# Pieces of a split exponential in single buffers, some of them made in place by an accumulating DMA, in a kernel for gated full and sliding-window attention

## The chip, the core and the metric

The kernel runs on one core of a Trainium2 chip. It is written for five engines: TensorE (PE: matmuls), VectorE (DVE), ScalarE (ACT: exponentials), GpSimd (POOL) and SyncE (SP, which issues DMA transfers). Data lies in SBUF (128 partitions); matmuls write to PSUM, which has eight banks of 512 float32 columns. The metric is the device time of one execution in microseconds, the median over several.

## The reference

Inputs are one sequence x of 2048 rows of 512, two sets of attention weights A and B, and a gate vector. All are bfloat16; there are 32 heads of 16 columns.

```python
x = A_x
g = sigmoid((x * gate_w).sum(-1, keepdims=True))
# A: full attention
qkv = (x @ A_wqkv).reshape(B, S, 3, H, Dh) ...
p = softmax(einsum("bhqd,bhkd->bhqk", q, k) * Dh ** -0.5)
a = einsum("bhqk,bhkd->bhqd", p, v).reshape(B, S, D) @ A_wo
# B: each row sees 8 keys, 2 rows apart, at and before itself
b = ... @ B_wo
out = g * a + (1 - g) * b
```

Nearly all of the work is in A: 32 heads with 2048 x 2048 scores each, whose exponentials are needed.

## The kernel before

**Items and blocks.** A's scores are cut into 2048 items. An item is one head, 128 keys and 512 queries: one matmul of 128 x 512 scores into one PSUM bank, 128 x 512 exponentials, and then one or more matmuls with V (with a column of ones beside it, which gives the softmax's denominator). Four heads run side by side on the four strips of the PE array. 64 items are a block (four heads, one stretch of 512 queries, 16 key tiles); there are 32 blocks. At a block's end its accumulator bank is normalised (`norm_steps`), and later the output projections follow (`outproj_specs`, and `outproj_last` for the last two tiles of rows).

**Two ways to make an exponential.** ACT takes items two or three banks at a time from two PSUM slots (banks 0 to 2 and 3 to 4): L1926 writes the tile `pt`, and one matmul per item with V follows (L1645, `pt,vaug`). The third bank of the wide slot can be lent out, and then ACT's exponential has two banks. DVE takes single items of certain key tiles (`KD`) in the remaining banks, by a sum of three pieces. A piece is a linear map of the score, written as int16 and read by PE as fp16, which makes a piecewise linear power of two; the three pieces are shifted against each other by thirds of an octave, and V is multiplied beforehand by the weights `PW_W` (tiles `vaug`, `vaugw`). So such an item has three matmuls with V, which sum in PSUM.

**How the three pieces are made.** DVE makes piece 0 from PSUM, item by item (`exp_dve`, L1564). Up to four items form a batch. When a batch is closed (`close_batch`), pieces 1 and 2 of the whole batch are made from piece 0 by adding an integer constant: on DVE (L1573) or on POOL (L1571, which adds two int16 at a time as int32, to a constant in the tile `pc`). The tile `yb` holds all three pieces of a batch; there are three such tiles (`NYB`), and one comes free when all of its 12 matmuls with V are done.

**Who decides the order.** The whole kernel is laid out when it is built. `run` keeps an estimate of the time on each engine (`t`), with a cost for each kind of step (`T_ACT`, `T_D1`, `T_D4`, `T_PI` and so on), and at each point picks what the engine that is furthest behind does next: the score matmuls of the next slot, matmuls with V whose pieces are thought ready, or another step (projections, branch B, output projections). Each engine then runs its instructions in that order, and semaphores make it wait where something isn't ready. The picks depend on limits: `TUNE` has places and due times in items, and `LEVELS` with `STRETCH` give twelve limits a level in each of 64 stretches of the run.

**Branch B** is spread through the same order: projections, logits by products and matmuls, and from some 375 us on transfers (`er`, `erb`, `vw`, issued by SP) and products on POOL (L1360). POOL also does the scaling of V (L930), part of the normalisation (L1678) and, early, squares of x (L1180). It issues two transfers: `woB` (L1153) and `woA`, which lies in the tile `wAv` (L1151).

**POOL and DVE.** When the planner puts a step on POOL, it makes it wait for the last DVE step marked `port` (L1573 pieces, products), and it holds such DVE steps back while it believes POOL to be busy.

Of the kernel before, what the change touches and what calls it, by code (L numbers as in the profile page):

```python
# [9 lines left out]
ALU = mybir.AluOpType  # L10
# [3 lines left out]
F16 = mybir.dt.float16  # L14
# [26 lines left out]
PW_S = tuple(s - math.log2(3.127444) for s in (0.0, -0.3330078125, 0.3330078125))  # L41
NP_ = len(PW_S)
KD = (2, 4, 7, 9, 12, 14)
KZ = (9,)
# [3 lines left out]
NPT = (4, 4)  # L48
NYB = 3
NQM = 3  # L50
# [4 lines left out]

TUNE = dict(relL=64, dueL2=2040, R0=74, R1w=42, R1g=20, R2g=31, R3g=46, R3w=50, dueB=61, dueL=84, v2rel=79, v2step=21, v2due=91, krel=230, krel2=192, ahead=0.142, dueV=30, dueS=115, dueO=678, dlast=62, qrel=28, prelB=59, prodrel=-12)

LEVELS = dict(
    pool=(0.0, 0.4, 1.2, 2.5, 4.0),
    backlog=(0.758, 1.231, 1.61, 1.894, 2.273, 2.841, 3.788),  # L60
    backlog_s=(0.888, 1.442, 1.886, 2.219, 2.663, 3.329, 4.438),
    part_us=(0.6, 0.975, 1.275, 1.5, 1.8, 2.25, 3.0),
    misc_slack=(-32, -18, -12, -8, -4, 2, 16),
    urgent=(-25, -11, -5, -1, 3, 9, 23),
    fit=(0.0, 0.2, 0.3, 0.4, 0.5, 0.6, 0.8),
    port=(0.338, 0.549, 0.718, 0.845, 1.014, 1.268, 1.69),
    alone=(-8.973, -0.273, -0.123, 0.027, 0.177, 0.327, 9.027),
    grab=(1, 0, 2, 3, 4),
    lend=(1, 0, 2, 3, 4, 5, 6, 7),
    order=((-1, 0, 1, 2, 1), (-1, 1, 0, 2, 3), (-1, 0, 2, 1, 3), (-1, 0, 1, 2, 3), (1, 0, 1, 2, 3), (0, 0, 1, 2, 3), (1, 0, 2, 1, 3), (2, 0, 1, 2, 3)),  # L70
)
STRETCH = dict(
    pool="1343344333433432333333333333232333333333333330333301233333333333",
    backlog="3333333333133333333333333333633333663333433463333133346332333333",
    backlog_s="3330413333333333333333323333033331333333631333333333331333332333",
    part_us="6333115334333333333333333533333333333643633330333335333333363303",
    misc_slack="3336333333533323333333333333333333333033333323333333433333303333",
    urgent="3341331533633333332533333333333333333333333303333333230333033331",
    fit="3613335633413353333333330333333111333333333340323333031333133333",
    port="3333533433333333333333332333333333435333333333333333333533333333",  # L80
    alone="2333333333333303333323333313333335133533303333333333333333333333",
    grab="0004204000034000030000003000000000000300000040000000300000000300",
    lend="0001000200000010000000000600000000000000000000401000006000020000",
    order="3003600020460000000144002001060007000000600020000000500060072000",
)
# [636 lines left out]
T_P1 = lambda n: n / 390.0 + 0.2  # L722
T_PI = lambda n: n / 1150.0 + 0.12
T_P2 = lambda n: n / 470.0 + 0.065
MM = 0.216
# [29 lines left out]
class _Fast:  # L755
# [15 lines left out]
    def setup(self):  # L771
# [17 lines left out]
                   for a, (w, n) in enumerate(zip(ACT_W, NPT))]  # L789
        self.yb = [c([P, NP_, YB_ITEMS * 512], I16, name=f"yb{i}") for i in range(NYB)]  # L790
        self.oT = [c([P, S], BF16, name=f"oT{i}") for i in range(2)]
# [76 lines left out]
        nc.gpsimd.memset(self.halo[:], 0.0)  # L868
        for k in range(1, NP_):
            nc.gpsimd.memset(self.pc[:, k:k + 1], round(1024.0 * (PW_S[k] - PW_S[0])) * 65537)  # L870
        self.idx = pidx, pf, ei, ef
# [616 lines left out]
    def run(self):  # L1488
# [17 lines left out]
        pt_refs = {}  # L1506
        yb_free = [0.0] * NYB
        batch = None
# [27 lines left out]
        def cold(now):  # L1536
            return sum(n for a, n in work if a > now - WARM_WIN) < WARM_BAR
# [23 lines left out]
        def exp_dve(slot_item):  # L1561
            (b, kt, j), bt, i, bank = slot_item
            A = SCALE * math.log2(math.e) * 1024.0
            return nc.vector.tensor_scalar(out=self.yb[bt["buf"]][:, 0, i * 512:(i + 1) * 512], in0=bank[:],  # L1564
                                           scalar1=A, scalar2=1024.0 * (15.0 + PW_S[0]), op0=ALU.mult, op1=ALU.add)

        def piece(bt, k, gp=False):
            n = len(bt["items"]) * 512
            y = self.yb[bt["buf"]]
            if gp:  # L1570
                return nc.gpsimd.tensor_tensor(out=y[:, k, 0:n].bitcast(I32), in0=y[:, 0, 0:n].bitcast(I32),  # L1571
                                               in1=self.pc[:, k:k + 1].to_broadcast([P, n // 2]), op=ALU.add)
            return nc.vector.tensor_scalar(out=y[:, k, 0:n], in0=y[:, 0, 0:n],  # L1573
                                    scalar1=float(round(1024.0 * (PW_S[k] - PW_S[0]))), scalar2=None, op0=ALU.add)

        def close_batch():
            nonlocal batch
            bt = batch
            batch = None
            n = len(bt["items"]) * 512  # L1580
            bt["refs"] = NP_ * len(bt["items"])
            parts = [dict(n=NP_) for _ in bt["items"]]

            def done(k, end):
                for i, it in enumerate(bt["items"]):
                    add_pv(it, self.yb[bt["buf"]][:, k, i * 512:(i + 1) * 512].bitcast(F16), end, ("y", bt, k), parts[i])
            now = min(t.values())
            pl = max(0.0, t["POOL"] - now) + sum(s.cost for s in self.steps if s.eng == "POOL" and s.rel <= p
                                                 and ready_time(s) <= now + 1.0)
            for k in range(1, NP_):  # L1590
                gp = pl < tune("pool") and n >= 1024
                pl += gp * T_PI(n)
                s = Step("POOL" if gp else "DVE", T_PI(n) if gp else T_D4(n), lambda k=k, gp=gp: piece(bt, k, gp),
                         deps=list(bt["p1"]), due=bt["due"], cls=2)
                s.on_done = lambda end, k=k: done(k, end)
                s.port = not gp
                self.steps.append(s)
            last = bt["p1"][-1]

            def after(end, prev=last.on_done):  # L1600
                prev(end)
                done(0, end)
            if last.end is None:
                last.on_done = after
            else:
                done(0, last.end)

# [8 lines left out]
        def emit_pv_one(j, now):  # L1616
# [13 lines left out]
            if kind == "p":  # L1630
                pt_refs[ref] -= 1
                if pt_refs[ref] == 0:
                    pt_free[ref] = now + 0.45
            else:
                ref["refs"] -= 1
                if ref["refs"] == 0:
                    yb_free[ref["buf"]] = now + 0.45
            out = self.flex[acc[b]][32 * j:32 * j + 32, :]
# [131 lines left out]
        def d_wanted(now, flex=True):  # L1770

            if p >= N - 8 or p % 64 >= TUNE["dlast"] or not any(k in KD for r in rem[p // 64] for k in r):
                return False
            if batch is None and min(yb_free) > now:
                return False
            if flex and min(fx_free) > now:
                return False
            ready = [s for s in self.steps if s.rel <= p and s.eng in ("PE", "DVE") and ready_time(s) <= now + TUNE["ahead"]]
            if flex and any(s.acq and s.due <= p + tune("misc_slack") for s in ready):
                return False  # L1780
            load = max(0.0, t["DVE"] - now) + sum(s.cost for s in ready if s.eng == "DVE")
            return load < tune("backlog" if flex else "backlog_s")
# [29 lines left out]
        def d_add(it, bank, p1done):  # L1812
# [3 lines left out]
            if batch is None:  # L1816
                buf = min(range(NYB), key=lambda i: yb_free[i])
                batch = dict(buf=buf, items=[], p1=[], due=0.0, blk=b)
                yb_free[buf] = INF
            bt = batch  # L1820
# [31 lines left out]
        def emit_alone(d, now):  # L1852
# [10 lines left out]
            d0.end = t["PE"] + 0.25  # L1863
            if batch is not None and p < N and p - 64 * batch["blk"] >= TUNE["dlast"]:
                close_batch()

        def emit_qk(dv, ac, now):
# [12 lines left out]
            for d in dv:  # L1880
                d[2].end = t["PE"] + 0.25
            if batch is not None and p < N and p - 64 * batch["blk"] >= TUNE["dlast"]:
                close_batch()
# [3 lines left out]
        while True:  # L1887
# [80 lines left out]
            else:  # L1968
# [27 lines left out]
                else:  # L1996
# [21 lines left out]
                    full = len(av) == 4  # L2018
                    part = av and (free_p <= 1 or min(yb_free) > now + 0.5 or cold(now) or now - old > tune("part_us") or (cur == NB - 1 and left[cur] <= len({(e[1], j) for j, q in enumerate(pvq) for e in q})) or p >= N)
                    pick = None  # L2020
# [93 lines left out]
```

## Time and profile before

| | |
|---|---|
| median of 3 runs | 703.62 us (702.6 to 704.75) |
| the profiled execution | 702.96 us |
| its span, first to last instruction | 701.2 us |
| mean granted clock of TensorE | 0.997 |
| exponentials on ACT: with 2 banks, with 3 banks | 582, 100 |
| items on DVE (L1564) | 584, mean 681 ns |
| pieces on DVE (L1573), on POOL (L1571) | 206, 104 |
| transfers that POOL issues | 2 |
| DMA, mean over the span | 69 GB/s |

How to read it: the span is what the sum of the prediction is made against. The busy time of an engine is the union of its instructions' spans, and a mean duration holds the time that an instruction spends beside its neighbour on the same engine. An arrow names who ended the idle time of an engine.

### The profile page before, as it was taken

What the parts mean: (1) busy time and instruction counts of PE and PEld (TensorE: products, weight loads), DVE (VectorE), ACT (ScalarE), POOL (GpSimd) and SP (SyncE); (2) the same over time, 40 slices, a digit from 0 to 9 for tenths busy, and PEclk for the clock granted to TensorE, in tenths of its full rate; (3) what the DMA queues carried; (4) which work ended last, traced back from release to release, by engine and by line L of the source; (5) the groups of instructions that cost most, each with busy time, mean ns of one, the idle gap of its engine ahead of it and who ended that gap; (6) DMA issues with size and microseconds to landing.
All of it is one profiled execution on the core that took longest, in us unless ns stands there. A gap on an engine that the chain in (4) does not pass through costs nothing.

```text
span 701.2 us, 21328 instructions
## 1 busy us (share of the span) xinstructions
PE 679.4 (97%) x8556; PEld 218.0 (31%) x8556; DVE 651.8 (93%) x1093; ACT 680.5 (97%) x696; POOL 429.1 (61%) x364
## 2 busy tenths in 40 slices
PE   9999999999999999999998999999999999999996
PEld 4432222233322232223332223322333232232343
DVE  6999999997899999999999899999999999989983
ACT  6999999999999999999999999999999999999995
POOL 4766877766476455555456666666567564576681
PEclk9999999999999999999999999999999999999999
DMA  6001101000100100000103236356463554566531
GB/s 175 5 16 36 45 3 31 2 2 9 35 2 15 26 1 5 6 2 9 34 1 92 99 79 165 106 146 162 96 156 97 149 134 112 128 167 173 136 84 36
DMA packets 64489, 48.70 MB, mean 69 GB/s; under 512 B 22528, under 2 KB 64000, under 8 KB 64256
## 3 DMA queue, kind: packets, MB, share of 16 engines
q1 hardware_dynamic: 63680, 45.83, 25.2%
q8 instruction: 69, 1.13, 0.7%
q0 software_dynamic: 288, 1.05, 0.5%
q10 hardware_dynamic: 416, 0.39, 0.2%
q14 instruction: 36, 0.29, 0.2%
HBM read 39.85 MB, written 5.26 MB: 64 GB/s over the span
## 4 chain that ended last, share of the span: by engine, by line
PE 60%; ACT 22%; issue 6%; DVE 5%; DMA 3%; SPq 2%; POOL 1%; ACTq 0%; DVEq 0%; POOLq 0%
ACT pt L1926 22%; PE fps L1872 21%; PE fps L1645 20%; PE fps L895 15%; DVE yb L1564 2%; DMA vw<-v_dram 1%; PE fps L1857 1%; SPq L1328 1%; PE fps L1378 1%; DVE yb L1573 1%; DMA erb<-er_dram 1%; DVE prod L1229 1%; SPq L968 1%; DMA x_in<-in_A_x_dram 1%; ACT er L1248 0%
## 5 line engine op out<-in xcount | busy, mean ns | idle before, releaser
L1926 ACT ACTIVATE pt<-fps 128x1024 bf16<-128x1024 f32 (+1 forms) x682 | 674.5, 1141 | 7.8 <-PE fps L1872 5.6
L1564 DVE TENSOR_SCALAR yb<-fps 128x512 int16<-128x512 f32 x584 | 377.8, 681 | 18.4 <-PE fps L1872 15.3
L1872 PE MATMUL fps<-qm,kT 32*128 32x512 bf16 x1976 | 285.9, 383 | 12.6 <-ACT pt L1926 7.8
L1645 PE MATMUL fps<-pt,vaug 128*32 128x512 bf16 (+1 forms) x1562 | 234.7, 373 | 0.4 <-DVE yb L1564 0.4
L1571 POOL TENSOR_TENSOR yb<-yb,pc 128x1024 int32<-128x1024 int32 (+1 forms) x104 | 188.4, 1822 | 64.6 <-DVE yb L1573 15.2
L1645 PE MATMUL fps<-yb,vaugw 128*32 128x512 f16 (+1 forms) x1228 | 174.6, 375 | 0.6 <-POOL yb L1571 0.4
L1872 PEld LDWEIGHTS <-kT 32*128 32x128 bf16 x1976 | 80.9, 91 | 272.2 <-issue 267.2
L1573 DVE TENSOR_SCALAR yb<-yb 128x2048 int16<-128x2048 int16 (+3 forms) x206 | 132.5, 670 | 0.6
L1645 PE MATMUL fps<-yb,vaug 128*32 128x512 f16 (+1 forms) x614 | 113.0, 375 | 0.0
L1360 POOL TENSOR_TENSOR er<-er,vw 128x512 bf16<-128x512 bf16 x64 | 72.8, 1156 | 49.7 <-DVE yb L1573 30.6
L895 PE MATMUL fps<-xT,ww 128*32 128x512 bf16 (+2 forms) x1296 | 99.5, 380 | 0.2
L1360 POOL TENSOR_TENSOR erb<-erb,vw 128x512 bf16<-128x512 bf16 x64 | 72.5, 1156 | 38.4 <-DVE yb L1573 20.6
L1645 PEld LDWEIGHTS <-vaug 128*32 128x32 bf16 x2176 | 64.8, 94 | 81.6 <-issue 74.7
L1645 PEld LDWEIGHTS <-vaugw 128*32 128x32 bf16 x1228 | 45.1, 94 | 41.8 <-issue 35.1
L1229 POOL TENSOR_TENSOR prod<-bq,bk 128x512 bf16<-128x512 bf16 x32 | 34.3, 1075 | 31.4 <-DVE yb L1573 17.4
L895 PEld LDWEIGHTS <-ww 128*32 128x32 bf16 x1296 | 25.8, 95 | 31.6 <-issue 23.8
L1678 POOL TENSOR_TENSOR t<-t,rc 128x512 bf16<-128x512 f32 x15 | 15.8, 1056 | 27.0 <-DVE yb L1573 12.2
L930 POOL TENSOR_SCALAR vaugw<-vaug 128x128 bf16<-128x128 bf16 (+1 forms) x24 | 20.4, 852 | 18.5 <-DVE vaug L923 10.8
L1857 PE MATMUL fps<-qm,kz 128*32 128x512 bf16 x288 | 30.8, 383 | 0.6 <-DVE yb L1564 0.4
L1229 DVE TENSOR_TENSOR prod<-bq,bk 128x2048 bf16<-128x2048 bf16 x24 | 29.9, 1271 | 0.2
L1668 DVE STREAM_TRANSPOSE t<-fps 128x512 f32<-128x512 f32 x32 | 22.7, 708 | 2.3 <-PE fps L1645 1.9
L895 PE MATMUL fps<-woB,oB 128*32 128x512 bf16 x256 | 19.9, 382 | 0.0
(117 smaller groups left out, 306.0 us busy)
## 6 DMA issues: line engine op xcount, KB each, us to landing
vw<-v_dram SPq DMA_DIRECT2D x128, 128.0 KB, 3.2
er<-er_dram SPq DMA_DIRECT2D x128, 64.0 KB, 3.3
erb<-er_dram SPq DMA_DIRECT2D x128, 64.0 KB, 2.9
v_dram<-vs SPq DMA_DIRECT2D x16, 128.0 KB, 2.6
qm<-qs SPq DMA_DIRECT2D x112, 16.0 KB, 1.8
out_dram<-ob SPq DMA_DIRECT2D x13, 128.0 KB, 2.7
x_in<-in_A_x_dram SPq DMA_DIRECT2D x3, 512.0 KB, 6.2
ww<-in_B_wqkv_dram SPq DMA_DIRECT2D x12, 128.0 KB, 2.8
```

Source lines behind the costliest of these rows:

```text
L895: self.nc.tensor.matmul(out=out_ps[32 * c:32 * c + 32, 0:n], lhsT=lhsT_of(c), rhs=rhs, start=start, stop=stop, tile_position=(0, 32 * c))
L930: return self.nc.gpsimd.tensor_scalar(out=self.vw4[k][:, KD.index(st), h0:h1, 0:DH], in0=self.vaug4[:, st, h0:h1, 0:DH], scalar1=PW_W[k], ...
L1229: return e.tensor_tensor(out=pr[m % 2][:, a:b], in0=bq[ct][:, a:b], in1=bk[ct][:, o + a:o + b], op=ALU.mult)
L1360: return nc.gpsimd.tensor_tensor(out=st_["erb"][m % 4][:, g, :], in0=st_["erb"][m % 4][:, g, :], in1=st_["vw"][m % 2][:, g, :], op=ALU.mult)
L1564: return nc.vector.tensor_scalar(out=self.yb[bt["buf"]][:, 0, i * 512:(i + 1) * 512], in0=bank[:], scalar1=A, scalar2=1024.0 * (15.0 + PW_ ...
L1571: return nc.gpsimd.tensor_tensor(out=y[:, k, 0:n].bitcast(I32), in0=y[:, 0, 0:n].bitcast(I32), in1=self.pc[:, k:k + 1].to_broadcast([P, n ...
L1573: return nc.vector.tensor_scalar(out=y[:, k, 0:n], in0=y[:, 0, 0:n], scalar1=float(round(1024.0 * (PW_S[k] - PW_S[0]))), scalar2=None, op0 ...
L1645: nc.tensor.matmul(out=out, lhsT=v, rhs=r, start=start, stop=stop, tile_position=(0, 32 * j))
L1668: nc.vector.transpose(out=self.t1[:, par].rearrange("p a b -> p (a b)"), in_=self.flex[acc[b]])
L1857: nc.tensor.matmul(out=dst[32 * c:32 * c + 32, :], lhsT=self.kz[:, j, KZ.index(kt), 32 * c:32 * c + 32], rhs=self.qm[(4 * ct + qc) % NQM][ ...
L1872: nc.tensor.matmul(out=dst, lhsT=self.kT[ct % 2][32 * j:32 * j + 32, kt * 128:(kt + 1) * 128], rhs=self.qm[(4 * ct + qc) % NQM][par][32 * ...
L1926: nc.scalar.activation(out=self.pt[pi[0]][pi[1]][:, 0:n * 512], in_=self.aslot[si][:, 0:n, :].rearrange("p a b -> p (a b)"), func=ACT.Exp, ...
```

## The change

The three-piece tile `yb` becomes eight single buffers `ys` of one piece of a batch each (`NSL`), and a constant tile `step` is added. DVE now makes the middle piece first (piece 1, by the shift `PW_S[1]`). The other two are made in one of two ways:

- fresh: a copy with a constant added into another buffer, on DVE or POOL, as before;
- in place: once every matmul and every copy that reads the buffer is done, POOL issues a DMA that adds the tile `step` to it (`accum_op=ALU.add`, 128 x 2048 int16, 512 KB for a full batch). The buffer then holds the next piece. A buffer can be changed twice so: piece 1, then 0, then 2, each step by the same constant.

How many of the two are fresh depends on the place in the block (the new limits `acc1`, `acc2`) and on the buffers that are free at that time: early in a block both can be made in place, later one, towards the end none. The planner counts such a transfer with 0.9 us on POOL, 1.8 in the queue for a full batch and 2.3 to its landing (5.0 from item 1100 on).

A batch is also closed at the very end of the items (`p < N` is dropped in two places). Ten values of `TUNE` and all of `LEVELS` and `STRETCH` are new, with fewer 3-bank exponentials and a different order throughout as a consequence. Branch B and the head and tail are changed only in their places.

```diff
+STEP_OF = {k: round(1024.0 * (PW_S[k] - PW_S[1])) for k in (0, 2)}
...
-NYB = 3
+NSL = 8
...
-TUNE = dict(relL=64, dueL2=2040, R0=74, R1w=42, R1g=20, R2g=31, R3g=46, R3w=50, dueB=61, dueL=84, v2rel=79, v2step=21, v2due=91, krel=230, krel2=192, ahead=0.142, dueV=30, dueS=115, dueO=678, dlast=62, qrel=28, prelB=59, prodrel=-12)
+TUNE = dict(relL=20, dueL2=2040, R0=110, R1w=42, R1g=12, R2g=31, R3g=43, R3w=50, dueB=61, dueL=84, v2rel=79, v2step=21, v2due=91, krel=230, krel2=214, ahead=0.142, dueV=-9, dueS=100, dueO=665, dlast=62, qrel=32, prelB=27, prodrel=-12)
 LEVELS = dict(
...
+    acc1=(-37, 11, 19, 27, 35, 43, 91),
+    acc2=(-57, -9, -1, 7, 15, 23, 71),
...
+ACC_B, T_ALB = 1100, 5.0
+T_AI, T_AQ, T_AL = 0.9, 1.8, 2.3
...
-        self.yb = [c([P, NP_, YB_ITEMS * 512], I16, name=f"yb{i}") for i in range(NYB)]
+        self.ys = [c([P, YB_ITEMS * 512], I16, name=f"ys{i}") for i in range(NSL)]
+        self.step = c([P, YB_ITEMS * 512], I16, name="step")
...
+        nc.gpsimd.memset(self.step[:].bitcast(I32), STEP_OF[0] * 65537)
...
+        def slice_dec(bt, sl, at):
+            bt["cnt"][sl] -= 1
+            bt["at"] = max(bt["at"], at)
+            if bt["cnt"][sl]:
+                return
+            if sl != bt["buf"] or not bt["ip"]:
+                ys_free[sl] = bt["at"] if sl == bt["buf"] else at
+                return
+            k = bt["ip"].pop(0)
...
+            def acc():
+                nonlocal acc_q
+                acc_q = max(acc_q, t["POOL"] + T_AI) + T_AQ * n / 2048
+                s.lat = acc_q + (T_AL if p < ACC_B else T_ALB) - t["POOL"] - T_AI
+                return nc.gpsimd.dma_start(out=self.ys[sl][:, 0:n], in_=self.step[:, 0:n], accum_op=ALU.add)
+            s = Step("POOL", T_AI, acc, deps=[d0], due=bt["due"], cls=2)
+            s.on_done = lambda end: bt["done"](k, sl, end)
...
+            pos = p - 64 * bt["blk"]
+            sls = sorted((i for i in range(NSL) if ys_free[i] <= now), key=lambda i: ys_free[i])[:NP_ - 1]
+            want = (pos >= tune("acc1")) + (pos >= tune("acc2"))
+            fresh = [2, 0][:min(len(sls), want)]
+            bt["ip"] = [k for k in (0, 2) if k not in fresh]
...
-            if batch is None and min(yb_free) > now:
+            if batch is None and sum(x <= now for x in ys_free) < 2:
...
-            if batch is not None and p < N and p - 64 * batch["blk"] >= TUNE["dlast"]:
+            if batch is not None and p - 64 * batch["blk"] >= TUNE["dlast"]:
```

## The prediction

> **What bounds the kernel now.** I read the page's busy shares first, then the groups by line and shape, then who waited for whom on ACT and PE, and last the rows around the two places where ACT stood still.
>
> ```profile
> span 701.2 us, 21328 instructions
> PE 679.4 (97%) x8556; PEld 218.0 (31%) x8556; DVE 651.8 (93%) x1093; ACT 680.5 (97%) x696; POOL 429.1 (61%) x364
> ...
> L1926 ACT ACTIVATE pt<-fps 128x1024 bf16<-128x1024 f32 (+1 forms) x682 | 674.5, 1141 | 7.8 <-PE fps L1872 5.6
> ```
>
> The groups by line with shapes kept apart (busy, mean ns of one, idle before):
>
> ```profile
> L1926 ACT ACTIVATE pt<-fps 128x1024 bf16<-128x1024 f32 x582 | 555.5, 1077 | 4.2 <-PE fps L1872 2.6 <-PE fps L1645 0.7 <-ACT pt L1926 0.2
> L1926 ACT ACTIVATE pt<-fps 128x1536 bf16<-128x1536 f32 x100 | 150.8, 1508 | 3.6 <-PE fps L1872 3.0 <-ACT pt L1926 0.2
> L1573 DVE TENSOR_SCALAR yb<-yb 128x2048 int16<-128x2048 int16 x178 | 121.8, 707 | 0.5
> L1571 POOL TENSOR_TENSOR yb<-yb,pc 128x1024 int32<-128x1024 int32 x94 | 176.8, 1891 | 59.5 <-DVE yb L1573 13.9 <-DVE yb L1564 13.5 <-PE fps L1872 10.2
> ```
>
> ACT's exponentials (L1926) fill 674.5 of 701.2 us with 7.8 us idle before them in the whole run. Neighbours overlap, so the mean of one is no price. The two widths differ by 1508 - 1077 = 431 ns, and 582a + 100(a + 0.431) = 674.5 gives a = 0.926 us for a two-bank exponential and 1.357 for a three-bank one. PE waits little for ACT (7.8 us at L1872), so the two are nearly level. DVE and POOL matter only where something of theirs comes late. The waits of ACT after the head are few:
>
> ```profile
> ACT pt L1926 <- PE fps L1872: 3.2, 7, 1.4
> ACT pt L1926 <- PE fps L1645: 0.7, 2, 0.3
> ACT pt L1926 <- ACT pt L1926: 0.4, 2, 0.2
> ```
>
> That is 4.3 us between 20 and 690 us. One event makes 1.97 of it:
>
> ```profile
> 384.50 0.40 PE L1872 MATMUL fps<-qm,kT 32*128 32x512 bf16 x4 [1.56 <-DVE yb L1564]
> 385.02 2.36 ACT L1926 ACTIVATE pt<-fps 128x1536 bf16<-128x1536 f32 x2 [0.59 <-PE fps L1872]
> ...
> 388.01 0.61 PE L1872 MATMUL fps<-qm,kT 32*128 32x512 bf16 x4
> 388.76 2.37 ACT L1926 ACTIVATE pt<-fps 128x1536 bf16<-128x1536 f32 x2 [1.38 <-PE fps L1872]
> ```
>
> PE waited 1.56 us for DVE. ACT lost 0.59 at once and 1.38 later, because PE's matmuls took 0.61 instead of 0.40 us for about 3 us (the granted clock is 0.83 in that slice of 10 us). A PE wait of that size costs ACT about 2 us.
>
> **The change, part by part.** Counts are from the built order of both programs, prices from rows.
>
> *ACT.* Two-bank exponentials go from 582 to 646, three-bank from 100 to 55, and one of one bank is new: 1464 banks become 1458, in 20 more instructions. 646 x 0.926 + 55 x 1.357 + 0.495 = 673.3, so -1.2 us. The last two exponentials shrink from three and two banks to two and one, which is 0.9 of that 1.2. On the path, up to the exponential that frees the bank for the last score matmul, only -0.3 is left.
>
> *The tail.* Behind the last score matmul PE had 64 matmuls of 512 columns and 52 of 256; now it has 112 and 20, as output projections have moved back. 16 matmuls take 1.05 us and 8 take 0.61, so one is 0.055 and a short one 0.0275: 4.95 us becomes 6.71, +1.76, all on the path. The normalisation of the last block (2.2 us on DVE) stays hidden behind 60 matmuls (3.3 us). Without them it would cost up to 2.2.
>
> *The head.* In the first 15 exponentials eight are of three banks instead of three. ACT lost 0.28 + 1.63 + 0.23 + 0.33 = 2.5 us there to PE's start-up work. Eight transposes (0.6 less 0.16 of switching, about 0.45 us) move from the 1.63 us gap to ahead of the first score matmul, so that part is a wash; the wider exponentials can cover the two small gaps. I take -0.5, bounds 0 and -2.5.
>
> *DVE.* Pieces made on DVE (L1573) fall from 206 to 153: 43 x 0.707 + 3 x 0.435 + 4 x 0.555 + 3 x 0.293 = 34.8 us less. Six more first exponentials (L1564) at 377.8/584 = 0.647 give back 3.9. DVE is 31 us lighter, and it is not the bound, so this counts only where PE waits for it. I take the event at 384 us as gone (-2.0); bounds 0 (it falls elsewhere) and -4.3 (every wait listed above).
>
> *POOL.* Its additions (L1571) fall by 33 x 1.891 + 3 x 1.464 + 3 x 1.037 = 69.9 us. New are 90 accumulating transfers, which POOL issues, and one memset of the step tile (about 1.0, like L860) in an idle stretch of the head. The nearest rows are the two plain 512 KB loads that POOL issues:
>
> ```profile
> 76.98 1.31 POOL L1153 DMA_DIRECT2D woB<-in_B_wo_dram  x1
> 77.29 0.69 DVE L1573 TENSOR_SCALAR yb<-yb 128x2048 int16<-128x2048 int16 x1
> 176.01 0.81 POOL L1151 DMA_DIRECT2D wAv<-in_A_wo_dram  x1
> ```
>
> and, from the list of transfers (KB each, us from issue to landing):
>
> ```profile
> woB<-in_B_wo_dram POOLq DMA_DIRECT2D x1, 512.0 KB, 4.6
> wAv<-in_A_wo_dram POOLq DMA_DIRECT2D x1, 512.0 KB, 4.6
> qm<-qs SPq DMA_DIRECT2D x112, 16.0 KB, 1.8
> ```
>
> 90 issues at 0.81 to 1.31 are 73 to 118 us, so POOL ends 3 to 48 us busier than 429 of 701, which its idle time covers.
>
> *The new wait.* An accumulation waits on POOL for the last matmul that reads the buffer. Queued behind it are branch B's products (er, erb), the normalisation product and the vaugw scaling, all 1.1 us pieces with due times many microseconds out. Its consumer is a probability-times-V matmul on PE, behind which the next score matmuls stand, and ACT behind those. So the question is whether the transfer lands before its consumer's turn. I counted, for each of the 90, the exponentials that stand between the releasing matmul and the consumer, at 0.926 and 1.357: 5.1 us for the tightest, seven of 5.6, two of 6.0, eleven of 6.4 to 6.5, six of 6.8 to 6.9, thirty others of up to 15.7 in the first half; 7.8 and up for the last 33. Lower price: 4.6, a plain load. Upper price: a 16 KB transfer lands in 1.8, so size made 2.8 of the 4.6; the accumulation also reads its destination, and doubling that part gives 7.4. I take 5.1, near the plain rows, since bytes and queue are the same: nobody is late, 0 us. At 7.4, 30 of the first 57 are late.
>
> A rule speaks against this. A load issued beside a DVE piece copy held POOL 1.31 us, one beside other DVE work 0.81: 0.50 us by the rows. The Trainium skill, page "SBUF — State Buffer", sections "SBUF: two separate sides" and "A bandwidth-pool intuition that's wrong (but worth ruling out)", says that VectorE in a two-port mode locks GpSimd out of writing descriptors, so that a transfer of 620 ns took 3100. An estimate by that page would put 2.5 us on each issue that meets such a copy, 7.1 instead of 5.1, and make those with the least slack 1 to 2 us late; the trace shows the effect at a fifth of that size.
>
> **Sum.** 701.2 - 0.3 + 1.76 - 0.5 - 2.0 + 0 = 700.2 us of span. The profiled execution took 702.96, 1.76 more than its span, and the median of the runs shown is 703.62, 0.66 above it: 700.2 + 1.76 + 0.66 = 702.6. The runs of before spread from 702.6 to 704.75; 0.3% (2.1 us) is about what a measurement of this kernel can tell from no change, so this is none.
>
> **The rivals.**
>
> *A: no change (0.36).* ACT's sum is equal to 0.2%, the tail's loss eats the head's and DVE's gain. For it: 4.3 us of idle time is all there is to win. Against: 90 new waits are unlikely to cost exactly nothing. 702.6, its own range 701.5 to 705.7.
>
> *B: faster (0.32).* With DVE 31 us lighter, nearly all of ACT's waits go: -4.3 instead of -2.0, and the head gives its -2.5. 701.2 - 0.3 + 1.76 - 2.5 - 4.3 = 695.9, so 698.3; half way there it is 700.4. For it: DVE stood at 49.6 of 50 us between 250 and 350 us, where its lateness starts. Against: those stretches have ACT at 50.0 of 50 already.
>
> *C: slower (0.32).* The accumulations land late and PE stands at their consumers. ACT has about one exponential (0.9 us) in hand, so it decides from a landing of 5.6 + 0.9 = 6.5 us after the release. At 7.4 the losses beyond 0.9 are 1.4 for the tightest, 7 x 0.9, 2 x 0.5 and next to nothing for the rest: 8.7 us, 708.9 in place of 700.2, or 711.3. Each PE wait near 1.5 us also risks the slower matmuls seen at 388 us, so more is possible. For it: the accumulating form is in no row, and POOL, in order, may be inside a 1.89 us addition when a buffer is released. Against: the slack listed, and loads of the same bytes at 4.6.
>
> *D: the change doesn't do what it says.* Then no accumulation would be in the order, but 90 of 308 pieces are. What is true of it is that they save ACT only six banks; the time would then be A's. It gets no chance of its own.
>
> **How the numbers follow.** A has the most and gives 702.6. B ends at 698.3 at its best, so the low end is 698. C at the upper price is 711.3; most of it lies under, and I put the high end at 710. That leaves out some 0.05 below and 0.13 above. Faster 0.32, same 0.36, slower 0.32 are B, A and C.
>
> **What would show it.** Right: the exponentials' group at 673 us; an interval of about 5 us from PE's last score matmul to ACT's closing copy growing to about 7; POOL's transfers landing in 4.6 to 5.5; no PE wait on them in the waits. Wrong: landings over 6.5, PE idle before L1690 put down to ys or to POOL, slices of granted clock under 1.0 beyond the one at 380 to 390 us, or ACT idle time after 20 us far from 2 us.

## The result and the profile after

The changed kernel takes 756.28 us (median of 4 runs, 754.23 to 761.15) against 704.18 (4 runs, 702.6 to 704.84): ratio 1.0753, 95% interval 1.0692 to 1.0815, so it is slower by 52 us. The prediction was 702.6 with a range up to 710. Its rival C, accumulations that land late, named a part of the mechanism and priced it far too low, at 711.3.

The page of the changed kernel is that of its slowest run (761.15 us). It shows its span, PE's busy share, the granted clock in 40 slices, the DMA queue of POOL (packets, MB, share), the groups of the exponentials, of the matmuls that read a buffer changed in place, and of the accumulations themselves (busy, mean ns | idle before), and their transfers (KB, us from issue to landing):

```profile
span 759.3 us, 21354 instructions
...
PE 706.2 (93%) x8531; PEld 219.9 (29%) x8531; DVE 642.2 (85%) x1046; ACT 686.9 (90%) x716; POOL 443.5 (58%) x416
...
PEclk9999999999999998999999999999989999898899
...
q0 software_dynamic: 13248, 47.19, 32.6%
...
L1971 ACT ACTIVATE pt<-fps 128x1024 bf16<-128x1024 f32 (+1 forms) x702 | 680.7, 1097 | 55.9 <-PE fps L1917 52.0
...
L1604 POOL DMA_DIRECT2D ys<-step x90 | 80.9, 954 | 55.8 <-PE fps L1917 31.7
...
L1690 PE MATMUL fps<-ys,vaug 128*32 128x512 f16 (+1 forms) x620 | 86.2, 387 | 22.6 <-DMA ys<-step 20.9
...
ys<-step POOLq DMA_DIRECT2D x86, 512.0 KB, 5.7
```

ACT was the bound and had 7.8 us of idle time before its exponentials. Now it has 55.9, and 52.0 of it is ended by a score matmul. PE in turn stands. Its waits in the changed kernel (total, times, longest):

```profile
PE fps L1690 <- DMA ys<-step: 21.4, 21, 2.7
...
PE fps L1917 <- DVE vs L1345: 4.2, 4, 2.0
```

The second row has a transfer behind it that is no accumulation. DVE writes the tile `vs` of branch B, and it stands until an earlier `vs` has been copied out; the kernel before has no such wait:

```profile
DVE vs L1345 <- DMA v_dram<-vs: 14.9, 7, 6.0
```

21 of the 90 accumulations make PE wait, 21.4 us in all, yet ACT loses more than twice that. One event shows how. POOL's rows, from when four accumulations follow each other (start, duration, idle before):

```profile
271.26 1.75 POOL L1604 DMA_DIRECT2D ys<-step  x2 [1.96 <-PE fps L1690]
273.88 0.85 POOL L1604 DMA_DIRECT2D ys<-step  x1 [0.87 <-DVE ys L1584]
...
275.43 1.19 POOL L1604 DMA_DIRECT2D ys<-step  x1
```

The first row holds two issues, at 271.26 and 271.84. The transfers issued at 271.84, 273.88 and 275.43 land 6.65, 7.3 and 9.71 us later. They share the engines, and the four landings are 2.7 to 4.0 us apart. The same stretch on PE:

```profile
281.22 0.40 PE L1690 MATMUL fps<-ys,vaug 128*32 128x512 f16 x4 [0.55 <-DMA ys<-step]
281.55 0.60 PE L1917 MATMUL fps<-qm,kT 32*128 32x512 bf16 x5
282.08 0.40 PE L1690 MATMUL fps<-pt,vaug 128*32 128x512 bf16 x4
285.18 0.62 PE L1690 MATMUL fps<-ys,vaug 128*32 128x512 f16 x4 [2.70 <-DMA ys<-step]
```

A row merges neighbouring instructions: the five of 281.55 take 0.38 us each. So after the wait of 0.55 us the matmuls keep their speed, and after that of 2.70 us they take about 0.6 us instead of 0.39, until 290.2. Two windows of 10 us (busy time of PE, weight loads, DVE, ACT, POOL; then granted clock, DMA share, GB/s):

```profile
270.00:280.00 10.00, 9.41 (x103) 2.88 (x101) 8.72 (x13) 9.68 (x10) 4.50 (x5) 1.00 1.02 191
280.00:290.00 10.00, 6.72 (x87) 1.89 (x85) 5.81 (x11) 6.38 (x8) 4.04 (x5) 0.68 0.61 117
```

In the first the DMA engines are full (1.02, 191 GB/s); in the second the clock is 0.68 and ACT works 6.38 of 10 us. So a PE wait of this length is paid twice, once standing and once slow.

**A measure for all runs.** From each exponential's start to the next one's I subtract a fixed step, 0.916 us for two banks and 1.343 for three (the median steps of the kernel before are 0.904 and 1.331). What is left is ACT's excess; other fixed steps would shift all rows nearly alike. Before it is 16.8 us in all, after 72.2. The sum of fixed steps is nearly equal (666.5 and 665.6). Adding the first exponential (+1.6 us later) and the stretch behind the last one (+2.5), these four terms give the span's +58.1 within 0.5: 55.4 of it is excess. It lies in both halves of the run:

| run | time, us | ratio (95%) | fixed steps | excess before 400 us | from 400 us | PE waits for accumulations |
|---|---|---|---|---|---|---|
| before | 704.2 | 1 | 666.5 | 13.5 | 3.4 | - |
| after | 756.3 | 1.0753 (1.0692 to 1.0815) | 665.6 | 31.2 | 41.0 | 21.4 |
| e1_sixteen | 708.7 | 1.0067 (1.0047 to 1.0087) | 665.6 | 13.9 | 5.0 | 0 |
| e2_plain | 727.7 | 1.0323 (1.0285 to 1.0361) | 665.6 | 14.1 | 26.5 | 1.7 |
| e4_late_small | 724.1 | 1.0278 (1.0256 to 1.0300) | 665.6 | 32.7 | 4.2 | 11.9 |
| e4_early_small | 741.0 | 1.0527 (1.0505 to 1.0549) | 665.6 | 13.8 | 38.6 | 9.7 |
| e5_fresh | 727.0 | 1.0329 (1.0303 to 1.0356) | 678.3 | 14.5 | 5.8 | - |
| e6_honest | 756.7 | 1.0753 (1.0725 to 1.0781) | 683.2 | 17.4 | 32.9 | 0.4 |
| e7_early | 727.4 | 1.0342 (1.0299 to 1.0386) | 680.5 | 18.2 | 3.7 | 0.7 |
| e8_wide | 770.1 | 1.0945 (1.0916 to 1.0974) | 686.7 | 14.2 | 42.9 | 0 |
| e9_self_late | 714.2 | 1.0141 (1.0122 to 1.0160) | 666.5 | 14.3 | 13.4 | - |
| e9_self_early | 705.3 | 1.0008 (0.9998 to 1.0018) | 666.5 | 14.1 | 3.5 | - |
| e10_old_limits | 734.7 | 1.0430 (1.0413 to 1.0448) | 680.1 | 16.5 | 11.9 | - |

### The profile page after: what moved, and what is told of

The parts are those of the page before. It is cut to its first block, busy times and chain, and to the rows that moved or that the text cites. A ratio compares the mean times of both kernels' runs of the same rounds, so it can differ in the third digit from the quotient of the medians.

```text
span 759.3 us, 21354 instructions
## 1 busy us (share of the span) xinstructions
PE 706.2 (93%) x8531; PEld 219.9 (29%) x8531; DVE 642.2 (85%) x1046; ACT 686.9 (90%) x716; POOL 443.5 (58%) x416
## 3 DMA queue, kind: packets, MB, share of 16 engines
q0 software_dynamic: 13248, 47.19, 32.6%
## 4 chain that ended last, share of the span: by engine, by line
PE 43%; DMA 23%; ACT 13%; DVE 9%; issue 4%; POOL 3%; SPq 3%; ACTq 0%; POOLq 0%; DVEq 0%
PE fps L1917 15%; PE fps L1690 14%; DMA ys<-step 13%; ACT pt L1971 13%; PE fps L905 11%; DVE ys L1575 4%; DMA vw<-v_dram 4%; DMA v_dram<-vs 3%; DMA erb<-er_dram 2%; DVE ys L1584 2%; DMA er<-er_dram 2%; SPq L1364 1%; SPq L1338 1%; POOL ys L1604 1%; PE fps L1388 1%
## 5 line engine op out<-in xcount | busy, mean ns | idle before, releaser
L1971 ACT ACTIVATE pt<-fps 128x1024 bf16<-128x1024 f32 (+1 forms) x702 | 680.7, 1097 | 55.9 <-PE fps L1917 52.0
L1575 DVE TENSOR_SCALAR ys<-fps 128x512 int16<-128x512 f32 x590 | 381.6, 680 | 50.4 <-PE fps L1917 45.6
L1917 PE MATMUL fps<-qm,kT 32*128 32x512 bf16 x1987 | 298.8, 392 | 17.4 <-ACT pt L1971 5.2
L1690 PE MATMUL fps<-pt,vaug 128*32 128x512 bf16 (+1 forms) x1556 | 228.6, 381 | 0.3 <-DVE ys L1575 0.2
L1690 PE MATMUL fps<-ys,vaugw 128*32 128x512 f16 (+1 forms) x1240 | 192.1, 381 | 2.6 <-DVE ys L1584 1.4
L1582 POOL TENSOR_TENSOR ys<-ys,pc 128x1024 int32<-128x1024 int32 (+1 forms) x65 | 123.3, 1898 | 75.8 <-DVE ys L1575 22.9
L1604 POOL DMA_DIRECT2D ys<-step x90 | 80.9, 954 | 55.8 <-PE fps L1917 31.7
L1584 DVE TENSOR_SCALAR ys<-ys 128x2048 int16<-128x2048 int16 (+3 forms) x153 | 108.2, 729 | 1.5
L1690 PE MATMUL fps<-ys,vaug 128*32 128x512 f16 (+1 forms) x620 | 86.2, 387 | 22.6 <-DMA ys<-step 20.9
L1345 DVE CAST vs<-fps 128x512 bf16<-128x512 f32 x16 | 11.0, 686 | 17.1 <-DMA v_dram<-vs 14.9
```

Source lines behind the costliest of these rows:

```text
L1575: return nc.vector.tensor_scalar(out=self.ys[bt["buf"]][:, i * 512:(i + 1) * 512], in0=bank[:], scalar1=A, scalar2=1024.0 * (15.0 + PW_S[1 ...
L1582: return nc.gpsimd.tensor_tensor(out=dst.bitcast(I32), in0=src.bitcast(I32), in1=self.pc[:, k:k + 1].to_broadcast([P, n // 2]), op=ALU.add)
L1584: return nc.vector.tensor_scalar(out=dst, in0=src, scalar1=float(STEP_OF[k]), scalar2=None, op0=ALU.add)
L1604: return nc.gpsimd.dma_start(out=self.ys[sl][:, 0:n], in_=self.step[:, 0:n], accum_op=ALU.add)
L1690: nc.tensor.matmul(out=out, lhsT=v, rhs=r, start=start, stop=stop, tile_position=(0, 32 * j))
L1917: nc.tensor.matmul(out=dst, lhsT=self.kT[ct % 2][32 * j:32 * j + 32, kt * 128:(kt + 1) * 128], rhs=self.qm[(4 * ct + qc) % NQM][par][32 * ...
```

## The experiments

**The size of the transfer.** The order of every instruction stays; only the accumulation is cut.

```diff
-out=self.ys[sl][:, 0:n], in_=self.step[:, 0:n], accum_op=ALU.add
+out=self.ys[sl][0:16, 0:n], in_=self.step[0:16, 0:n], accum_op=ALU.add
```

> The same order and the same waits as the changed kernel, but each of the 90 accumulations touches 16 of the 128 partitions (64 KB instead of 512 KB), so the other rows miss the addition. Theory 1 (the transfers' size: they land later than the order allows, PE stands at their readers, and its clock falls): landing under 4 us, no wait of PE on ys<-step, 703 to 712 us. Theory 2 (the new limits and order lose the time by themselves: head, tail, POOL holding up DVE): still 740 us or more. In between, both: head and tail alone, by the trace of the changed kernel, are some 8 us.

708.68 us: 47.6 of the 52 us are gone with seven eighths of the bytes (the step is added on 16 of 128 partitions). No matmul waits for an accumulation any more, the clock is 0.999, and the excess before 400 us is within 0.4 of that of the kernel before. So the transfers are the cause and the order is not, up to the last 4 us. They come mostly at the ends: first exponential +0.75, excess +2.1, behind the last one +2.6. POOL's 90 issues at L1604 and its waits for PE ahead of them are all still there, so they are not what costs.

**Plain or accumulating.**

```diff
-in_=self.step[:, 0:n], accum_op=ALU.add
+in_=self.step[:, 0:n]
```

> The same order, waits and size, but a plain copy of the step tile instead of an accumulation (the pieces made in place are then wrong). If the second read of the destination makes the transfer late: landing 4.6 us instead of a median of 5.7, and most of the 52 us gone (705 to 715). If the bytes or the issue are the cost, whatever the kind: 745 us or more.

727.73 us, 28.5 less than the changed kernel, between the two ranges expected. A plain copy of the same bytes (it overwrites the piece with the step) lands in 3.8 us (median) instead of 5.7, and the packets of POOL's queue take 18.3% of the 16 engines' span instead of 32.6%. The early half is clean with it, 14.1 against 31.2, but the late half still has 26.5, 23 more than the kernel before. So early the extra time of the accumulation decides, and late the bytes alone do most of the damage.

**Which half.** Small transfers only after item 1100, or only before it.

```diff
+q = 16 if p >= ACC_B else P        # e4_late_small
+q = 16 if p < ACC_B else P         # e4_early_small
-out=self.ys[sl][:, 0:n], in_=self.step[:, 0:n], accum_op=ALU.add
+out=self.ys[sl][0:q, 0:n], in_=self.step[0:q, 0:n], accum_op=ALU.add
```

> The accumulations from item 1100 on touch 16 partitions, the earlier ones all 128 (the rows left out miss the addition). In the changed kernel ACT stood some 27 us of its extra idle time behind 400 us, where landing times reach 15 us beside branch B's loads. Theory 1a (lateness in the quiet first half is the main cost): 730 us or more. Theory 1b (the collision with branch B's transfers behind item 1100 is the main cost): 715 to 728.

> The reverse: accumulations before item 1100 touch 16 partitions, the later ones all 128. Theory 1a: 710 to 728. Theory 1b: 730 us or more. If the two parts are independent, the gains of this kernel and of the one with small late transfers add up to that of the kernel with all of them small.

Small late ones save 32.2 us, small early ones 15.2, together 47.4 of 47.6: the halves add up and don't work on each other. 57 accumulations cost 15 us before item 1100, and 33 cost 32 after it, three to four times as much each.

**Without accumulations, and with the transfers' measured times in the plan.** Two explanations were left. Lateness: a consumer is placed before its transfer lands, because the plan's durations are too short. Collision: the bytes delay other transfers, whether their own consumer waits or not. Four kernels with new orders; where both pieces are always fresh (in e5, and in e7 from item 1100 on), a batch also opens only with three buffers free instead of two:

```diff
-want = (pos >= tune("acc1")) + (pos >= tune("acc2"))
+want = 2                                        # e5_fresh; NSL = 9, no step tile
+want = 2 if p >= ACC_B else (pos >= ...         # e7_early, with the constants of e6
-ACC_B, T_ALB = 1100, 5.0
-T_AI, T_AQ, T_AL = 0.9, 1.8, 2.3
+ACC_B, T_ALB = 1100, 8.0                        # e6_honest; 12.0 in e8_wide
+T_AI, T_AQ, T_AL = 0.9, 2.8, 2.5                # e6, e7; 0.9, 2.8, 5.0 in e8_wide
```

> No accumulation at all: both outer pieces always go to a buffer of their own by an ordinary addition, a batch opens only with three buffers free, and the memory of the step tile becomes a ninth buffer; the new limits stay. The planned order has 632 exponentials of 1024 columns, 74 of 1536 and one of 512; at the cadences of the trace before (0.916 us and 1.343 us) that is 678.3 us on ScalarE against 667.4 for the kernel before, so +11. Theory 1 (the loss of the changed kernel is TensorE standing for accumulations that land late): the waits at L1690 for a DMA are gone, clock above 0.995, and the time is the kernel before plus 11 for ScalarE plus about 4 for head and tail: 719 us, 712 to 726. Theory 2 (single buffers and new limits starve ScalarE by themselves, the accumulations only show it): over 735, with the excess between exponentials above 30 us.

> The planner's three constants for an accumulation are set nearer to what the trace showed: 2.8 us per queued transfer instead of 1.8, landing 2.5 us after its turn instead of 2.3 (6.2 us from issue in all instead of 5.0), 8.0 instead of 5.0 in the second half (11.7 us in all). 73 accumulations remain of 90. Planned exponentials 608 of 1024 and 95 of 1536, 684.5 us on ScalarE by the cadences of before, +17. Theory 1 (lateness against the plan): TensorE's waits for accumulations fall from 21 us to under 6, clock above 0.99, time 704 + 17 + 4 + up to 6 = 725 to 733. Theory 2 (the transfers hurt by what they collide with, not by being late against the plan): 73/90 of the loss stays on top of ScalarE's 17, over 745.

> As the run with measured constants, but accumulations only before item 1100 (49 of them); after it both outer pieces are always ordinary additions. Planned exponentials 608 of 1024 and 93 of 1536, 681.8 us on ScalarE, +14. Theory 1: 704 + 14 + 4 + up to 4 = 722 to 728, no wait for an accumulation after 400 us of the span. Theory 2 (collisions): early half alone cost 15 us beyond the order, so 49/57 of that stays: over 733.

> A wide margin: 2.8 us per queued transfer, 5.0 after its turn in the first half (8.7 us from issue) and 12.0 in the second (15.7 us). 81 accumulations. Planned exponentials 628 of 1024, 83 of 1536, one of 512: 686.7 us on ScalarE, +19. Theory 1: hardly a consumer is held by a landing (TensorE's waits for accumulations under 3 us), clock above 0.995: 704 + 19 + 4 = 727, 722 to 732. Theory 2 (collisions): 81 accumulations still cost most of 47 us on top of the order: over 755.

*e5_fresh*: 727.02, one us above theory 1's range. +11.8 of ACT's work as planned, +3.6 of excess, +1.0 at the start, and the stretch behind the last exponential 6.6 longer, where 4 was put for head and tail together. Theory 2 is out: the excess is 20.4 in all.

*e7_early*: 727.39, inside theory 1's 722 to 728. The 49 early accumulations are still of full size, and the waits for them are nearly gone (3 of 0.7 us in all).

*e6_honest* and *e8_wide* fell out of theory 1, at 756.7 and 770.1 instead of 725 to 733 and 722 to 732, though in its early half it was right: 17.4 and 14.2 us of excess against 31.2. The late half loses 32.9 and 42.9 us while PE waits 0.4 and 0 us for accumulations. In e8 the largest stall is put down to a small transfer of branch B, `kz<-kT` (8 KB). SP's row:

```profile
593.67 4.74 SPq L984 DMA_DIRECT2D kz<-kT  x4
```

and PE's, where the matmuls that read it stand, and ACT's:

```profile
602.68 0.62 PE L1902 MATMUL fps<-qm,kz 128*32 128x512 bf16 x4 [7.56 <-DMA kz<-kT]
...
604.41 1.02 ACT L1971 ACTIVATE pt<-fps 128x1024 bf16<-128x1024 f32 x1 [8.06 <-PE fps L1917]
```

Three accumulations had been issued from 589.14 to 592.8, all with a margin that their consumers didn't use up. The four `kz` transfers took 4.74 us to issue (1.15 each on the average; 0.57 in the kernel before) and landed after 7.4 us (median; 1.8 before). From 400 us on `vw<-v_dram` reaches 9 in 10 of its landings within 4.2 us before and 6.3 in e8; `er<-er_dram` 3.8 and 5.3. In e7, with e6's constants and no late accumulation, the late excess is 3.7. So theory 2 holds late, theory 1 early.

The margins cost as well. A buffer that is held longer is a batch that DVE doesn't take, and ACT's fixed steps go to 683 to 687 us.

**The collision by itself.** The kernel before, in its own order, with 27 plain copies of `woB` onto itself that nobody consumes at that time:

```diff
+while extra and p >= extra[0]:
+    extra.pop(0)
+    nc.gpsimd.dma_start(out=self.woB[:], in_=self.woB[:])
+extra = [1100 + 20 * i for i in range(27)]      # e9_self_early: 300 + 20 * i
```

> The kernel before, in its own order, with 27 extra transfers of 512 KB that nobody consumes: from item 1100 on, every 20 items, POOL issues a copy of the output weights woB onto themselves in SBUF (they are first read at item 1700 or so). Theory collision (in the second half the bytes on the 16 DMA engines delay branch B's own transfers, whose readers then stand, whether or not an accumulation is itself late): the plain copies of the changed kernel cost some 24 us between 400 and 700 us with 33 transfers, so 27 cost 12 to 24: 716 to 728, with waits on vs, vw, er or kz. Theory lateness (only a consumer that stands for an accumulation costs): nothing consumes these, 703 to 708.

> The same 27 copies, with the same issues on POOL, but from item 300 on, where the kernel has hardly a transfer of its own. Theory collision: 703 to 708, as there is nothing to collide with; the difference to the late run is the price of the collision. Theory lateness: as the late run, 703 to 708. If the issues on POOL (27 of some 0.85 us) are what costs, both runs rise alike, by up to 23 us.

Early: 705.27, an interval that includes no change, and each copy lands in 3.1 us:

```profile
woB<-woB POOLq DMA_DIRECT2D x27, 512.0 KB, 3.1
```

Late: 714.22, +9.9, all of it excess after 400 us, and the same copy takes 5.1:

```profile
woB<-woB POOLq DMA_DIRECT2D x27, 512.0 KB, 5.1
```

Lateness of a consumer can't do this, as there is none; issues on POOL by themselves don't, as the early run has as many, and e1 has 33 late ones with 5.0 us of excess. The waits of the late run on `vs`, and on the copies themselves:

```profile
PE fps L1873 <- DVE vs L1335: 1.7, 1, 1.7
DVE vs L1335 <- DMA v_dram<-vs: 1.7, 1, 1.7
POOL woB L1958 <- DMA woB<-woB: 5.0, 4, 2.9
```

The first two are one event at 488 us, and ACT loses 3.5 us in it and just behind it: branch B's transfer is the victim there. The third is a rival within this run: POOL stands for its own earlier copy, which never happens in the early run. Behind the longest of these waits PE stands 0.85 us for a piece from POOL, and ACT loses 0.9. How much of the 9.9 us comes this way beyond that isn't known.

The cost is less than the 12 to 24 expected. The 33 plain copies of e2 cost 23 us late (26.5 less 3.4): 0.7 each against 0.37 here. Here the copies come evenly every 20 items, and the kernel before has other transfers at other times. Which of the two makes the difference wasn't tried.

**The limits.**

```diff
-TUNE, LEVELS and STRETCH of the changed kernel (in e5_fresh)
+TUNE, LEVELS and STRETCH of the kernel before
```

> Single buffers (nine, no accumulation, both outer pieces ordinary additions) with the limits of the kernel before: the buffers alone. The planned order has 568 exponentials of 1024 columns, 119 of 1536, one of 512, 680.6 us on ScalarE by the cadences of before, +13. Theory 1 (limits belong to one plan; a batch now opens with three single buffers free instead of one whole one, and nothing but ScalarE's share changes): 704 + 13 = 717, 714 to 721. Theory 2 (single buffers gain by themselves because they come free earlier): 704 or less.

734.67: both theories missed. ACT's fixed steps are +13.6, as counted. Beyond that 8.1 us of excess fall between 650 and 700 us, and the stretch behind the last exponential is 7.6 longer. Single buffers without accumulations brought nothing here. With the new limits (e5) the same buffers take 727.0, so limits fitted to one order can be worth several us less in another; but e10, like the kernel before, also doesn't close a batch at the very end of the items, and that wasn't tried apart.

No version tried here beats the kernel before. With an eighth of the bytes, which leaves most of the additions out, its order takes 708.7.

## Why the prediction was wrong

*ACT, -0.3 us.* Right that there is next to nothing to win. The sum of fixed steps is 0.9 smaller, but that is counted, not measured: with small transfers the exponentials' group is busy for 674.5 us, as in the kernel before, against the 673.3 predicted.

*The tail, +1.76.* Right in kind. From the last score matmul to ACT's closing copy it is 5.54 us before and 7.02 after, +1.48; behind the copy another 0.3 to 0.5 came on top.

*The head, -0.5.* Wrong sign. The first exponential is 0.75 us later in e1, where the eight transposes now stand ahead of the first score matmul. The wider exponentials didn't cover the rest: in e1 two POOL additions lie over the gate's steps on DVE.

```profile
27.89 3.92 POOL L1582 TENSOR_TENSOR ys<-ys,pc 128x1024 int32<-128x1024 int32 x2 [3.07 <-DVE ys L1575]
...
28.11 1.95 DVE L1149 TENSOR_SCALAR eg<-eg 128x512 f32<-128x512 f32 x1 [0.31 <-ACT eg L1144]
...
32.97 1.02 ACT L1971 ACTIVATE pt<-fps 128x1024 bf16<-128x1024 f32 x1 [2.04 <-PE fps L1917]
```

The same step took 0.63 us in the kernel before, beside a shorter scaling on POOL. It ends late, DVE's copies of V behind it too, and ACT stands for 2.04 us.

*DVE's relief, -2.0.* Right: in e1 the excess from 350 to 400 us falls from 2.8 to 0.6.

*POOL's issues hidden.* Right: mean 0.954 us, within the 0.81 to 1.31 taken; the longest is 1.85. None took the 2.5 us of the prediction's estimate.

*Accumulations, 0 us; rival C 8.7.* This is the step that failed; it cost 47.6. Four things in it:

- The room was counted from the release of the buffer by its last matmul. POOL issues 1.2 us after it (median, first 57; one in ten over 4.2) and 5.4 us (last 33; one in ten over 16). From issue to landing the first 57 take 5.4 us; in e1, where nobody waits, the consumers come about 5.2 us after the issue (landing after 3.2, matmul 2.0 later). The room was gone at the median.
- The landing was bounded by 4.6 and 7.4, from transfers that were alone. The tile's own row of the changed kernel goes beyond:

```profile
DMA to landing us min/median/max: 4.5/5.7/15.2
```

  The fastest is near the 4.6 of the plain row, but the sum's 5.1 is under the median. The long ones come behind each other, as at 275.43 us, and beside branch B's: the first 57 take 9.7 us at most, and the 15.2 is among the last 33.
- The price of a wait was its excess over 0.9 us. PE's slow matmuls after it were mentioned and left out of the sum; ACT lost 17.8 us early for 12.2 us of waits on accumulations, and 37.6 late for 9.2.
- No rival had transfers as victims. Branch B's own transfers were named only as what POOL has to do besides. They count in the larger part: 32 of 47.6 us come after item 1100, and two orders with 0.4 and 0 us of waits for accumulations lose 30 and 39 us there.

How the 32 us divide in the changed kernel itself isn't settled. e4_early_small has 9.7 us of waits for late accumulations and 35 us of excess over the kernel before; in the changed kernel itself PE stands 9.2 us for late accumulations and 5.9 for DVE's `vs`, so both are at work.

## What to carry to other kernels

Before a transfer takes over an engine's work, count its room from the issue to the reader, not from the moment its buffer is free, and price it with its neighbours in flight, not alone. Then ask whose transfers run in that stretch: bytes that nobody waits for can stop an engine through somebody else's small load. Try the new order once with small transfers and once with the transfers alone in the old order; the two together tell lateness from collision.

## What the runs showed of the hardware

An accumulating transfer of 512 KB within SBUF landed in 4.5 us at the least, a plain one in 3.1 (median of e9_self_early, in a stretch with little other traffic). The Trainium skill, page "DMA: Bandwidth & Descriptors", section "Anatomy of one DMA — SWDGE (gpsimd) path", gives 2.0 us plus bytes over 436 GB/s, an estimate of 3.2 us here: it fits the plain copy, and the fastest accumulation takes 1.3 us more. The same page of the Trainium skill, section "Issuing engines are not separate DMA queues", says that transfers of all issuing engines run interleaved on the same 16 engines, and the late copies agree (5.1 instead of 3.1 us, and branch B's landings longer).

A PE wait of 2.70 us was followed by matmuls of about 0.6 us instead of 0.39 and a granted clock of 0.68 over 10 us; one of 0.55 us was not. The Trainium skill, page "TensorE: Matmul & The Clock Gate", section "HAM oscillation — how this bites in real kernels", warns of idle gaps above some 3.4 us; here a shorter one was enough.

A step on DVE (128 x 512, float32) took 1.95 us beside two integer additions on POOL, and 0.63 in the kernel before.
